# Token order of q in a linear-attention and SoLU kernel: runs of eight tokens on 64 partitions per head

## The chip, the cores and the metric

The kernel runs on one core of one Trainium2 chip. A core has five engines with queues of their own: TensorE (PE, matrix products), VectorE (DVE), ScalarE (ACT), GpSimd (POOL) and SyncE (SP). SP, ACT and POOL can issue transfers, which 16 shared DMA engines carry out. Weight loads of PE (PEld) are recorded beside its products. The metric is the time of one execution on the device, in microseconds (us), lower is better.

## What is computed

The inputs are q, k and v of 8 batches, 8 heads, 576 tokens and 64 values each, a norm weight, and the two matrices of an expert layer. Everything is float32 in and out.

```python
# attention without a softmax, then a norm over the 64 values of each head
kv  = np.einsum('bhsd,bhse->bhde', k, v)
out = np.einsum('bhsd,bhde->bhse', q, kv)
rms = np.sqrt(np.mean(out * out, axis=-1, keepdims=True) + 1e-06)
attn = out / rms * g_norm
# tokens x (heads * 64) = 4608 x 512, through 512 -> 1024 -> 512
x = attn.transpose(0, 2, 1, 3).reshape(B * S, H * D)
h = x @ w_in
sm = np.exp(h - h.max(-1)) / sum(...)
solu = h * sm
ln = (solu - mean(solu)) / sqrt(var(solu) + 1e-06) * g_ln
y = ln @ w_out
```

Every token passes through the two parts by itself, apart from kv, which sums over all tokens of its batch and head. So the order in which tokens sit in the kernel's chunks is free, as long as each row of the output ends up at its own place.

## The kernel before

**Chunks.** The 4608 tokens are worked in nine chunks of 512. Chunks c = 0 to 7 hold tokens 0 to 511 of batch c. Chunk 8 holds the last 64 tokens of all eight batches. The feature dimension lies on the partitions for the expert layer, the tokens on the free dimension.

**Loading.** `load_kv` (line 213) brings k and v of a batch as bf16: a pair of heads fills the 128 partitions, 64 for each, and a partition holds nine tokens that follow each other. `load_q` (line 222) brings tokens 0 to 511 of q with 128 partitions, each holding four tokens of every head (`j=4`). `load_q_last` (line 230) brings the last 64 tokens of one batch, on every eighth partition of the tile `q_last`. All these are issued by POOL, which casts on the way. Batches 0 and 1 are loaded in two halves of four heads.

**Attention.** `kv_mm` (line 280) forms kv from k and v, `kv_copy` brings it to SBUF as `kvd`, once straight and once with the two halves of the partitions exchanged. q has to be transposed, so that head values lie on partitions: for chunks 0 to 3 by `qT_mm` (line 313), eight 128x128 products against an identity per half, with `qT_copy`; for chunks 4 to 8 (`XBAR`) by `q_turn` (line 330), one DMA transpose issued by SP. A transposed block of 128 rows holds two tokens: z = 0 on partitions 0 to 63, z = 1 on the others. `o_mm` (line 337) forms q times kv for half the heads (`hf`), with two results (z) of 512 columns. For chunks 0 to 7 that is eight products of 256 columns per half. For chunk 8 it is 64 products of 32 columns per half, since each batch needs its own kv and its columns are every eighth one. Then come a square (`o_sq`), the mean over a head by a product (`s_mm`), the root (`s_ln`, `s_exp`) and the scaling `x_mul`.

**Expert layer.** For every chunk `h_mm` makes eight blocks of h (four products of 512 columns each), `h_exp` (ACT) and `h_u` (DVE) the exponential and the product with it. POOL and ACT make the squares and sums that `sums` (PE) reduces. `out_mm` (line 578) makes four blocks of 128 tokens by 512 outputs, in half steps of four products; `scale` (line 609) multiplies by the row's factor and writes `ob`, of which there are four buffers in turn; `store` (line 616) sends 128 rows of 2 KB out. Stores go on SP's queue, except that in chunk 8 block 1 goes on ACT's. Block 3 of chunk 8 is made in two column halves (`out_cols`, `scale_cols`, `store_cols`, lines 587 to 607), one stored by SP and one by ACT.

**The order of the work** is written by a planner (`Plan`, line 19). Every piece is given an engine, a cost, a rank (a due time), what it needs and which buffers it takes. `order` then picks, again and again, the piece that could start first by these costs, and by rank among equals. The engines run their lists strictly in that order. So a changed cost or rank, as in `plan.add(("q_last", b), ...)` (line 266), can move other pieces too. The SP list before is: four stores of chunk 0, the transpose of chunk 4, three stores of chunk 1, the transpose of chunk 5, four stores, that of 6, three stores, that of 7, four stores, that of 8, and the other stores.

Of the kernel before, what the change touches and what calls it, by code (L numbers as in the profile page):

```python
# [8 lines left out]
FP32 = mybir.dt.float32  # L9
FP32R = mybir.dt.float32r  # L10
BF16 = mybir.dt.bfloat16
# [78 lines left out]
def kernel(  # L90
# [20 lines left out]
    nc = tc.nc  # L111
    B, H, S, D = q.shape
# [34 lines left out]
    kvd = big.tile([128, B, 2, NP, D], BF16, name="kvd")  # L147
    q_last = big.tile([128, H, 4, D], BF16, name="q_last")
    g_rep = big.tile([128, 1], FP32, name="g_rep")
# [62 lines left out]

    def load_kv(name, src, b, hs):

        if hs.start == 0:
            T[name, b] = tile_of((name, b), [128, NP, 9, D], BF16)
        nc.gpsimd.dma_start(  # L217
            T[name, b].rearrange("p n i d -> p n (i d)")[:, hs.start // 2:hs.stop // 2],
            src[b, hs].rearrange("(n r) (p i) d -> (r p) n (i d)", r=2, i=9),
        )  # L220

    def load_q(b, hs):
        if hs.start == 0:
            T["q", b] = tile_of(("q", b), [128, H, 4, D], BF16)
        nc.gpsimd.dma_start(  # L225
            T["q", b].rearrange("p h j d -> p h (j d)")[:, hs],
            q[b, :, 0:512, :].rearrange("h (p j) d -> p h (j d)", j=4)[:, hs],
        )

    def load_q_last(b):  # L230
        nc.gpsimd.dma_start(
            q_last[b:128:B].rearrange("p h j d -> p h (j d)"),
            q[b, :, 512:S, :].rearrange("h (p j) d -> p h (j d)", j=4),
        )

# [16 lines left out]
    for b in range(B):  # L252
        at = b - 9.0 if b > 1 else (-2.0, -1.5)[b]
        behind = [] if b < 2 else [("h_mm", 0, 0)] if b == 2 else [("h_mm", b - 3, 2 if b == 3 else 0)]
        for g, hs in enumerate(heads(b)):
            part = 0.1 * g
            n = len(heads(b))
            for i, (name, src) in enumerate((("k", k), ("v", v))):
                plan.add((name, b, g), "pool", 0.75 if n == 1 else 0.6, at + part + 0.01 * i,
                         lambda name=name, src=src, b=b, hs=hs: load_kv(name, src, b, hs),  # L260
                         behind, uses=[(name, b)] if g else [],
                         first=[] if g else [(name, b)], load=2.9 / n if b < 3 else 3.5)
            plan.add(("q", b, g), "pool", 0.9 if n == 1 else 0.7, at + part + (0.02 if b < 2 else 0.1),
                     lambda b=b, hs=hs: load_q(b, hs), behind,
                     uses=[("q", b)] if g else [], first=[] if g else [("q", b)], load=2.7 / n if b < 3 else 3.3)
        plan.add(("q_last", b), "pool", 0.6, 2.0 + 0.5 * b, lambda b=b: load_q_last(b),
                 [("h_mm", 2 + b // 2, 4 * (b % 2))], load=0.5)
    for half in range(2):
# [44 lines left out]
    def qT_mm(c, hf, tag):  # L313

        t = T["qTp", c, hf] = bank((tag,), [128, 4, 2, 128], BF16)
        for h in range(4):
            for y in range(2):
                src = T["q", c][:, 4 * hf + h, 2 * y:2 * y + 2, :].rearrange("p z d -> p (z d)")
                nc.tensor.transpose(t[:, h, y, :], src, ident[:, :])

    def qT_copy(c, hf):
        if hf == 0:
            T["qT", c] = tile_of(("qT", c), [128, H, 2, 128], BF16)
        dst, src = T["qT", c][:, 4 * hf:4 * hf + 4], T["qTp", c, hf][:, :, :, :]
        if c == 1:
            nc.scalar.copy(dst, src)
        else:
            nc.vector.tensor_copy(dst, src)

    def q_turn(c):  # L330

        t = T["qT", c] = tile_of(("qT", c), [128, H, 2, 128], BF16)
        nc.sync.dma_start_transpose(
            t.rearrange("q h y p -> q (h y) p"), T["q", c].rearrange("p h j d -> p (h j d)")
        )

    def o_mm(c, hf, tag):

        ts = [bank((tag,), [128, 2, 2, 128], FP32) for z in range(2)]
        for z in range(2):  # L340
            T["o", c, hf, z] = ts[z]
        for pp in range(2):
            for b in [c] if c < B else range(B):
                cols = slice(0, 128) if c < B else slice(b, 128, B)
                for hh in range(2):
                    for z in range(2):
                        rows = slice(64 * z, 64 * z + 64)
                        nc.tensor.matmul(  # L348
                            ts[z][hh * 64:hh * 64 + 64, pp, :, cols], kvd[rows, b, hh ^ z, 2 * hf + pp, :],
                            T["qT", c][rows, 4 * hf + 2 * pp + hh, :, cols], start=True, stop=True,  # L350
                        )
# [23 lines left out]
    def s_exp(*i):  # L375
        t = T["rst", i] = tile_of(("rst", i), [128, 2, 2, 128], FP32)
        nc.scalar.activation(  # L377
            out=t.rearrange("p a b c -> p (a b c)"), in_=T["lss", i][:, :], func=AF.Exp, scale=-0.5, bias=zero_t[:, :]
        )

    def s_rsqrt(*i):
        t = T["rst", i] = tile_of(("rst", i), [128, 2, 2, 128], FP32)
        nc.scalar.activation(
            out=t.rearrange("p a b c -> p (a b c)"), in_=T["s", i][:, :], func=AF.Abs_reciprocal_sqrt, bias=eps_t[:, :]
        )

    def x_mul(c, hf, z):
        if (hf, z) == (0, 0):
            T["x", c] = tile_of(("x", c), [128, NP, 2, 2, 128], BF16)
        nc.vector.scalar_tensor_tensor(  # L390
# [6 lines left out]
    for c in range(NC):  # L397
# [19 lines left out]
        for hf in range(2):  # L417
            g = group(c, hf)
            tag = ("out", "h")[c] if c < 2 and hf else "o"
            if c not in XBAR:  # L420
# [8 lines left out]
            kvs = [("kv", b, x, part) for b in ([c] if c < B else range(B)) for x in ((hf,) if b < 2 else range(2)) for part in range(3)]  # L429
            plan.add(("o_mm", c, hf), "pe", 0.25 if c < B else 1.2, r + w * (0.35 + 0.5 * hf),  # L430
                     lambda c=c, hf=hf, tag=tag: o_mm(c, hf, tag), [("qT", c) if c in XBAR else ("qT", c, hf), *kvs],
# [173 lines left out]
    def store_cols(x):  # L605
        dst = out.rearrange("(b s) (x d) -> b s x d", b=B, x=2)[:, 512:S, x, :].rearrange("b (p j) d -> j p b d", j=4)[3]
        (nc.sync, nc.scalar)[x].dma_start(dst, T["ob", NC - 1, 3][:, x])

    def scale(c, m):
# [3 lines left out]
        else:  # L613
            nc.vector.tensor_scalar_mul(out=t[:, :], in0=T["acc", c, m][:, :], scalar1=T["rstd", c][:, m:m + 1])  # L614

    def store(c, m):
        j = 2 * (m % 2) + m // 2
        if c < B:
            dst = out[c * S:c * S + 512, :].rearrange("(p j) d -> j p d", j=4)
        else:  # L620
            dst = out.rearrange("(b s) d -> b s d", b=B)[:, 512:S, :].rearrange("b (p j) d -> j p b d", j=4)

        (nc.scalar if c == NC - 1 and m % 2 else nc.sync).dma_start(dst[j], T["ob", c, m][:, :])

# [65 lines left out]
```

## Time and profile before

| | us |
|---|---|
| median of 6 runs | 196.23 |
| lowest and highest of them | 195.36, 205.79 |
| the profiled execution | 195.36 |
| its span, first to last instruction | 193.6 |
| PE busy | 180.5 |
| ACT busy | 141.1 |
| POOL busy | 128.0 |
| DVE busy | 122.3 |

The granted TensorE clock was 1.0 throughout. Busy time of PE is modelled with overlapping ends, so the time that a group of products holds PE is better read from its start to the start of the next group. The chain that ended last gives 27% of the span to `out_mm` (L582) and 25% to `h_mm` (L468).

What the loads look like from POOL's side and on the DMA queues:

```profile
L225 POOL DMA_DIRECT2D q_sb<-in_q_dram x10 | 8.6, 856 | 2.5 <-DMA w_in_sb<-in_moe_w_in_dram 1.4
```

```profile
q0 software_dynamic: 20112, 17.30, 56.6%
q1 hardware_dynamic: 15616, 11.67, 23.1%
```

The first row is a group of instructions: line, engine, operation, tile, count, then busy time, mean ns of one, idle time before it and what ended most of it. The next two are the DMA queue of POOL (q0) and that of SP (q1): packets, megabytes, share of the 16 engines' span.

```profile
out_dram<-ob_sb SPq DMA_DIRECT2D x34, 256.0 KB, 3.1
q_sb<-in_q_dram POOLq DMA_DIRECT2D x6, 512.0 KB, 16.0
q_last<-in_q_dram POOLq DMA_DIRECT2D x8, 64.0 KB, 10.0
qT_sb<-q_sb SPq DMA_TRANSPOSE x4, 9.6
```

These rows are transfers: how many, KB each, and the median us from issue to landing.

### The profile page before, as it was taken

How to read it: one execution, taken by the hardware profiler on the slowest of the kernel's cores; microseconds unless marked ns; L12 is line 12 of the kernel's file. 1: busy time of each engine (PE TensorE's matmuls, PEld its weight loads, DVE VectorE, ACT ScalarE, POOL GpSimd, SP SyncE). 2: the span in 40 equal slices, each digit the busy share in tenths (PEclk: the TensorE clock that was granted, in tenths of full speed). 3: DMA queues.
4: the chain of work that ended last, by engine and by line, in shares of the span. 5: the costliest groups of instructions: out<-in, count | busy, mean ns of one | idle time of the engine just before them, and what ended most of it. 6: DMA issues, size and time to landing. Idle time of an engine off the chain costs nothing.

```text
span 193.6 us, 5442 instructions
## 1 busy us (share of the span) xinstructions
PE 180.5 (93%) x2282; PEld 88.7 (46%) x2282; DVE 122.3 (63%) x241; ACT 141.1 (73%) x245; POOL 128.0 (66%) x136
## 2 busy tenths in 40 slices
PE   7987997997999998999799999999999999999991
PEld 2442454652354533544254435445445554544460
DVE  1356588478684886496377668577575747666450
ACT  2028888879895996899588987979789496655420
POOL 7982699400999986977489776568385838846200
PEclk9999999999999999999999999999999999999999
DMA  3999999999995999999999997353111111211206
GB/s 47 193 203 279 342 203 206 205 224 254 228 205 83 128 164 268 134 175 185 274 214 195 210 82 208 113 102 129 54 54 58 58 54 58 108 58 54 110 11 210
DMA packets 36040, 29.71 MB, mean 153 GB/s; under 512 B 11816, under 2 KB 30512, under 8 KB 36016
## 3 DMA queue, kind: packets, MB, share of 16 engines
q0 software_dynamic: 20112, 17.30, 56.6%
q1 hardware_dynamic: 15616, 11.67, 23.1%
q8 instruction: 18, 0.29, 0.6%
q10 hardware_dynamic: 288, 0.39, 0.6%
q14 instruction: 6, 0.05, 0.1%
HBM read 32.51 MB, written 9.44 MB: 217 GB/s over the span
## 4 chain that ended last, share of the span: by engine, by line
PE 71%; ACT 9%; DMA 8%; DVE 4%; POOL 3%; issue 2%; SPq 0%; POOLq 0%; DVEq 0%
PE out_ps L582 27%; PE h_ps L468 25%; PE misc_ps L534 4%; DMA out_dram<-ob_sb 4%; DMA v_sb<-in_v_dram 4%; PE s_ps L369 3%; PE o_ps L348 3%; ACT e_sb L476 2%; PE misc_ps L291 2%; DVE u_sb L483 2%; ACT osq_sb L363 2%; ACT rst_sb L377 1%; ACT lss_sb L373 1%; POOL k_sb L217 1%; DVE w_out_sb L573 1%
## 5 line engine op out<-in xcount | busy, mean ns | idle before, releaser
L468 PE MATMUL h_ps<-x_sb,w_in_sb 128*128 128x512 bf16 x276 | 70.3, 379 | 2.8 <-DVE u_sb L483 1.5
L582 PE MATMUL out_ps<-w_out_sb,u_sb 128*128 128x512 bf16 x272 | 69.1, 379 | 0.7 <-issue 0.7
L494 POOL TENSOR_TENSOR usq_sb<-u_sb 128x512 bf16<-128x512 bf16 x50 | 52.0, 1043 | 26.6 <-DVE u_sb L483 26.5
L483 DVE TENSOR_TENSOR u_sb<-h_ps,e_sb 128x512 bf16<-128x512 f32 x69 | 47.4, 689 | 30.3 <-ACT e_sb L476 29.4
L500 POOL TENSOR_TENSOR es_sb<-e_sb 128x512 bf16<-128x512 f32 x36 | 45.9, 1274 | 21.8 <-ACT e_sb L476 21.4
L476 ACT ACTIVATE e_sb<-h_ps,zero_t 128x512 f32<-128x512 f32 x69 | 47.2, 685 | 12.5 <-PE h_ps L468 11.6
L468 PEld LDWEIGHTS <-w_in_sb 128*128 128x128 bf16 x288 | 27.3, 98 | 37.3 <-issue 6.7
L582 PEld LDWEIGHTS <-u_sb 128*128 128x128 bf16 x280 | 26.1, 98 | 31.6 <-issue 2.7
L363 ACT ACTIVATE osq_sb<-o_ps,zero_t 128x512 bf16<-128x512 f32 x31 | 20.2, 684 | 15.7 <-PE o_ps L348 15.7
L614 DVE TENSOR_SCALAR ob_sb<-out_ps,rstd 128x512 f32<-128x512 f32 x33 | 24.6, 746 | 10.7 <-PE out_ps L582 4.5
L390 DVE SCALAR_TENSOR_TENSOR x_sb<-o_ps,g_rep,rst_sb 128x512 bf16<-128x512 f32 x32 | 23.9, 749 | 8.6 <-ACT rst_sb L377 8.4
L377 ACT ACTIVATE rst_sb<-lss_sb,zero_t 128x512 f32<-128x512 f32 x32 | 23.2, 726 | 0.7
L373 ACT ACTIVATE lss_sb<-s_ps,eps_t 128x512 f32<-128x512 f32 x32 | 22.0, 689 | 2.0 <-PE s_ps L369 1.9
L492 ACT ACTIVATE usq_sb<-u_sb,zero_t 128x512 bf16<-128x512 bf16 x22 | 15.8, 719 | 5.4 <-DVE u_sb L483 5.4
L369 PE MATMUL s_ps<-osq_sb,head_mean 128*128 128x512 bf16 x34 | 12.9, 380 | 0.6 <-ACT osq_sb L363 0.6
L534 PEld LDWEIGHTS <-stat_sel 128*32 128x32 bf16 x720 | 10.1, 97 | 3.8 <-issue 3.8
L198 PE MATMUL s_ps<-zeros 128*128 128x512 bf16 x28 | 9.9, 480 | 1.4 <-DVE zero_t L163 1.2
L217 POOL DMA_DIRECT2D k_sb<-in_k_dram x10 | 7.8, 785 | 3.6 <-DMA w_in_sb<-in_moe_w_in_dram 2.2
L225 POOL DMA_DIRECT2D q_sb<-in_q_dram x10 | 8.6, 856 | 2.5 <-DMA w_in_sb<-in_moe_w_in_dram 1.4
L348 PE MATMUL o_ps<-qT_sb,kvd 64*64 64x32 bf16 (+1 forms) x240 | 8.2, 256 | 1.8 <-DMA qT_sb<-q_sb 1.3
L291 PEld LDWEIGHTS <-k_sb 64*64 64x64 bf16 x576 | 6.8, 107 | 4.0 <-issue 4.0
L348 PEld LDWEIGHTS <-kvd 64*64 64x64 bf16 x256 | 4.6, 114 | 8.3 <-issue 7.3
(85 smaller groups left out, 134.7 us busy)
## 6 DMA issues: line engine op xcount, KB each, us to landing
out_dram<-ob_sb SPq DMA_DIRECT2D x34, 256.0 KB, 3.1
k_sb<-in_k_dram POOLq DMA_DIRECT2D x6, 576.0 KB, 14.1
v_sb<-in_v_dram POOLq DMA_DIRECT2D x6, 576.0 KB, 14.7
q_sb<-in_q_dram POOLq DMA_DIRECT2D x6, 512.0 KB, 16.0
w_out_f<-in_moe_w_out_dram POOLq DMA_DIRECT2D x1, 2048.0 KB, 15.8
k_sb<-in_k_dram POOLq DMA_DIRECT2D x4, 288.0 KB, 11.2
v_sb<-in_v_dram POOLq DMA_DIRECT2D x4, 288.0 KB, 11.9
q_sb<-in_q_dram POOLq DMA_DIRECT2D x4, 256.0 KB, 11.9
```

What stands on the lines that cost most here:

```text
L363: nc.scalar.activation(out=t[:, :], in_=T[("o", *i)].rearrange("p a b c -> p (a b c)"), func=AF.Square, bias=zero_t[:, :])
L369: nc.tensor.matmul(t[:, :], head_mean[:, :], T["osq", i][:, :], start=True, stop=True)
L373: nc.scalar.activation(out=t[:, :], in_=T["s", i][:, :], func=AF.Ln, bias=eps_t[:, :])
L377: nc.scalar.activation(out=t.rearrange("p a b c -> p (a b c)"), in_=T["lss", i][:, :], func=AF.Exp, scale=-0.5, bias=zero_t[:, :])
L390: nc.vector.scalar_tensor_tensor(out=T["x", c][:, 2 * hf:2 * hf + 2, z], in0=T["o", c, hf, z][:, :, :, :], scalar=g_rep[:, :], in1=T["rst" ...
L468: nc.tensor.matmul(t[:, :], w_in_sb[:, dt, f * 128:(f + 1) * 128], T["x", c][:, dt].rearrange("p a b c -> p (a b c)"), start=(dt == 0), st ...
L476: nc.scalar.activation(out=T["e", c, f // 2][:, f % 2, :], in_=T["h", c, f][:, :], func=AF.Exp, bias=zero_t[:, :])
L483: nc.vector.tensor_tensor(out=T["u", c][:, f, :], in0=T["h", c, f][:, :], in1=T["e", c, f // 2][:, f % 2, :], op=MUL)
L494: nc.gpsimd.tensor_tensor(out=dst, in0=src, in1=src, op=MUL)
L500: nc.gpsimd.tensor_tensor(out=T["es", c][:, n, :], in0=e[:, 0, :], in1=e[:, 1, :], op=ADD)
L582: nc.tensor.matmul(T["acc", c, m][:, :], T["u", c][:, f, m * 128:(m + 1) * 128], w_out_sb[:, f, :], start=(f == 0), stop=(f == NF - 1),)
L614: nc.vector.tensor_scalar_mul(out=t[:, :], in0=T["acc", c, m][:, :], scalar1=T["rstd", c][:, m:m + 1])
```

## The change

q is now laid out as k and v are: a pair of heads fills the partitions, 64 for each, and a partition holds eight tokens that follow each other; one `load` serves all three. The ninth token of every partition goes to chunk 8. There, the batch stands where the token of the run stood before: `q_last[:, :, b, :]`, one token of each partition and head pair for each batch. `o_mm` takes four runs of 64 columns instead of two of 128; in chunk 8 it makes 32 products of 64 columns per half, where y and z name the batch. The loads of last tokens become due late (rank 4.0 + 0.25 b) and wait for later steps of `h_mm`. A block of 128 rows of the output now holds two tokens of every run (for chunk 8: two batches), and each store is two of 64 rows.

```diff
-    q_last = big.tile([128, H, 4, D], BF16, name="q_last")
+    q_last = big.tile([128, NP, B, D], BF16, name="q_last")
...
+    def load(name, src, b, hs):
+        js = 8 if name == "q" else 9
         if hs.start == 0:
-            T[name, b] = tile_of((name, b), [128, NP, 9, D], BF16)
+            T[name, b] = tile_of((name, b), [128, NP, js, D], BF16)
         nc.gpsimd.dma_start(
+            T[name, b].rearrange("p n j d -> p n (j d)")[:, hs.start // 2:hs.stop // 2],
+            src[b, hs].rearrange("(n r) (p j) d -> (r p) n (j d)", r=2, j=9)[:, :, 0:js * D],
         )
-    def load_q(b, hs):
-        if hs.start == 0:
-            T["q", b] = tile_of(("q", b), [128, H, 4, D], BF16)
-        nc.gpsimd.dma_start(
-            T["q", b].rearrange("p h j d -> p h (j d)")[:, hs],
-            q[b, :, 0:512, :].rearrange("h (p j) d -> p h (j d)", j=4)[:, hs],
-        )
     def load_q_last(b):
-        nc.gpsimd.dma_start(
-            q_last[b:128:B].rearrange("p h j d -> p h (j d)"),
-            q[b, :, 512:S, :].rearrange("h (p j) d -> p h (j d)", j=4),
-        )
+        nc.gpsimd.dma_start(q_last[:, :, b, :], q[b].rearrange("(n r) (p j) d -> (r p) n j d", r=2, j=9)[:, :, 8, :])
...
-        plan.add(("q_last", b), "pool", 0.6, 2.0 + 0.5 * b, lambda b=b: load_q_last(b),
-                 [("h_mm", 2 + b // 2, 4 * (b % 2))], load=0.5)
+        plan.add(("q_last", b), "pool", 0.7, 4.0 + 0.25 * b, lambda b=b: load_q_last(b),
+                 [("h_mm", 4 + b // 4, 2 * (b % 4))], load=0.7)
...
-            for b in [c] if c < B else range(B):
-                cols = slice(0, 128) if c < B else slice(b, 128, B)
+            n = 2 * hf + pp
+            for y in [slice(0, 4)] if c < B else range(4):
                 for hh in range(2):
                     for z in range(2):
                         rows = slice(64 * z, 64 * z + 64)
                         nc.tensor.matmul(
-                            ts[z][hh * 64:hh * 64 + 64, pp, :, cols], kvd[rows, b, hh ^ z, 2 * hf + pp, :],
-                            T["qT", c][rows, 4 * hf + 2 * pp + hh, :, cols], start=True, stop=True,
+                            ts[z][hh * 64:hh * 64 + 64, pp, y, :], kvd[rows, c if c < B else 2 * y + z, hh ^ z, n, :],
+                            T["qT", c][rows, n, y, 64 * hh:64 * hh + 64], start=True, stop=True,
                         )
...
     def store_cols(x):
-        dst = out.rearrange("(b s) (x d) -> b s x d", b=B, x=2)[:, 512:S, x, :].rearrange("b (p j) d -> j p b d", j=4)[3]
-        (nc.sync, nc.scalar)[x].dma_start(dst, T["ob", NC - 1, 3][:, x])
+        cols = slice(x * d_model // 2, (x + 1) * d_model // 2)
+        for y in range(2):
+            (nc.sync, nc.scalar)[x].dma_start(
+                rows_of(NC - 1, 1, 2 + y)[:, cols], T["ob", NC - 1, 3][64 * y:64 * y + 64, x]
+            )
...
+    def rows_of(c, z, y):
+        if c < B:
+            return out[c * S:c * S + S, :].rearrange("(p j) d -> j p d", j=9)[2 * y + z]
+        return out.rearrange("(b p j) d -> j b p d", p=64, j=9)[8, 2 * y + z]
     def store(c, m):
-        j = 2 * (m % 2) + m // 2
...
-        (nc.scalar if c == NC - 1 and m % 2 else nc.sync).dma_start(dst[j], T["ob", c, m][:, :])
+        for x in range(2):
+            (nc.scalar if c == NC - 1 and m % 2 else nc.sync).dma_start(
+                rows_of(c, m // 2, 2 * (m % 2) + x), T["ob", c, m][64 * x:64 * x + 64, :]
+            )
```

The planner's costs follow: a q load counts 0.8 for POOL instead of 0.9 and 2.55 for DMA instead of 2.7 (3.2 instead of 3.3 from batch 3 on), half loads of q count 0.6 instead of 0.7, and the products of chunk 8 count 0.6 a half instead of 1.2. In the order that comes out, the last tokens' loads follow batch 7's loads, the loads of batches 5 and 6 stand one POOL instruction earlier, the transpose of chunk 6 stands one store earlier on SP and that of chunk 8 two stores later, and the steps of PE are mixed differently from chunk 1's end on.

## The prediction

> **What bounds the kernel now.** I read four views. First the page's slices and the table of busy time by stretch:
>
> ```profile
> PE   7987997997999998999799999999999999999991
> DMA  3999999999995999999999997353111111211206
> ...
> 88.00:96.00 8.00, 6.69 (x39) 2.88 (x37) 4.18 (x7) 5.76 (x9) 4.97 (x5) 1.00 1.29 216
> ...
> 112.00:128.00 16.00, 16.00 (x229) 7.74 (x230) 11.28 (x23) 14.28 (x26) 10.25 (x11) 1.00 0.60 116
> ...
> 144.00:160.00 16.00, 16.00 (x267) 8.38 (x265) 10.04 (x19) 12.02 (x22) 9.43 (x9) 1.00 0.14 51
> ```
>
> Columns of the last three: stretch, length, busy time (count) of PE, weight loads, DVE, ACT, POOL, granted clock, DMA share, GB/s. There are two regimes. Up to about 100 us the DMA engines are full (the 9s) and PE has holes. From 112 us on PE is busy without a hole while DMA falls to 0.60 and then 0.14. So after 100 us only TensorE work counts; before it, what DMA brings, and when, counts too.
>
> Second, the timeline of PE around the last chunk, with a kv product for comparison:
>
> ```profile
> 53.84 0.22 PE L291 MATMUL misc_ps<-v_sb,k_sb 64*64 64x64 bf16 x2
> ...
> 54.55 1.90 PE L468 MATMUL h_ps<-x_sb,w_in_sb 128*128 128x512 bf16 x8
> ...
> 144.83 1.13 PE L348 MATMUL o_ps<-qT_sb,kvd 64*64 64x32 bf16 x64
> 145.89 1.04 PE L582 MATMUL out_ps<-w_out_sb,u_sb 128*128 128x512 bf16 x4
> ```
>
> PE time is read from start to next start. The 64 small products of the last chunk's first half hold PE for 145.89 - 144.83 = 1.06 us (16.6 ns each), the second half 1.07 us (154.67 to 155.74). The 72 products of a kv step, with the same 64x64 weights and twice the columns, take 54.55 - 53.84 = 0.71 us: 9.9 ns each.
>
> Third, the chain of waits and the timeline at the one large hole:
>
> ```profile
> 86.94 0.50 SPq L333
> 87.53 8.33 DMA out_dram<-ob_sb
> 95.96 0.75 DVE ob_sb L614
> ```
>
> ```profile
> 80.53 6.90 SPq L333 DMA_TRANSPOSE qT_sb<-q_sb  x1
> 95.57 0.41 PE L348 MATMUL o_ps<-qT_sb,kvd 64*64 64x256 bf16 x8 [1.31 <-DMA qT_sb<-q_sb]
> ```
>
> Batch 5's DMA transpose could start only at 80.53, when q of batch 5 (issued at 62.82) had landed. It held SP for 6.90 us, and its data came at about 95.5, because k, v and q of batch 6 (issued from 78.34 on) share the engines. The product that needs it waited. A store behind it on SP took 8.33 us and held an output buffer. Eight output matmuls before that product took 95.57 - 92.37 = 3.20 us where eight take 1.73 elsewhere: 1.5 us lost.
>
> Fourth, ACT at the end:
>
> ```profile
> 187.59 0.69 ACT L612 ACTIVATE ob_sb<-out_ps,rstd 128x512 f32<-128x512 f32 x1 [1.12 <-PE out_ps L582]
> 188.31 0.63 ACTq L623 DMA_DIRECT2D out_dram<-ob_sb  x1
> 189.29 0.47 ACT L603 ACTIVATE ob_sb<-h_ps,rstd 128x256 f32<-128x256 f32 x1 [1.01 <-PE h_ps L592]
> 189.79 0.56 ACTq L607 DMA_DIRECT2D out_dram<-ob_sb  x1
> ```
>
> The last store leaves ACT's queue at 189.79 and lands 2.7 us later; the span ends at 193.6.
>
> **The change part by part.**
>
> *Last chunk's products.* Before, each of 8 batches has its own 16 tokens in two groups, 128 products of 32 columns read with a stride of 8. Now y runs over 4 and z picks the batch, so there are 64 products of 64 adjoining columns. Upper price: 32 a half at today's 16.6 ns is 0.53 us, saving 2 x 0.53 = 1.06 us. Lower price: 32 at the kv rate of 9.9 ns is 0.32 us, saving 2 x 0.75 = 1.5 us. I take 1.5: the kv row has the new form exactly (64x64 weights, 64 adjoining columns, all four quadrants in turn). Nothing covers it, as PE has no hole there: -1.5 us. For the other chunks the 256 columns become four runs of 64 instead of two of 128; the sums step reads runs of 32 at the usual rate, so nothing is added (if it slowed them by 10%, 16 steps of 0.34 us would cost 0.5 us).
>
> *Loads of q.* A half load goes from 512 pieces of 1 KB to 256 of 2 KB, a whole one from 1024 to 512. One half of q (512 pieces, 32 for each of 16 engines) took 13.41 - 12.03 = 1.38 us, from the landing of v in the chain to the end of PE's wait for q: 43 ns for a piece of 1 KB. k and v of the same half, 32 pieces of 2.25 KB per engine, came in the 3.0 us left of the 4.4 us between the two first kv steps (7.62 and 12.07), at most 95 ns each. A piece of 2 KB then costs 75 to 86 ns, and a whole q load shrinks by 0 to 0.4 us of about 8 us per batch. I take 0.2. At the start two halves stand ahead of the first expert matmul: -0.1 us. POOL's own issue (856 ns a q load) shrinks by some 0.1, hidden in its idle time.
>
> *Last tokens.* Eight loads move from between batches 5 to 7's loads to behind batch 7's, and each goes from 128 pieces (1 KB read, 512 B written) to 512 pieces (256 B read, 128 B written). The total goes from 1024 to 4096. On POOL an issue with 512 pieces takes 0.78 us (the half q loads) against 0.56: 8 x 0.22 = 1.8 us more, in a stretch where POOL is busy 10.25 of 16 us. Behind it wait squares and sums whose results are needed a chunk later: nothing, and up to 0.5 us if they become late. On DMA no row has 128 B writes. Nearest are the transposes: queue q1's 15616 packets less 4608 store rows leave some 2200 for each of five, 137 per engine, and the last one, with the engines nearly to itself, landed in 4.3 us: at most 31 ns a packet. So 32 x 31 ns = 1.0 us a load, 8 us in all. The Trainium skill, "DMA: Bandwidth & Descriptors", Specifications, speaks against it: a transfer below 512 B is a read-modify-write and misses line rate. If that doubled the price the eight would take 16 us. They fall between about 98 and 130 us, where DMA has a third of its time free, and the last transpose was issued at 127.42 and not needed until 144.83. I take the trace's price and zero on the path; the slack of 13 us is the cover, and beyond it each microsecond of landing is one of PE.
>
> *The planner.* The printed order shows that batch 5's and 6's loads each move ahead of a POOL square (1.0 us earlier); batch 6's transpose goes ahead of one store, and the last one behind two. Batch 5's first product comes after 23 half output steps instead of 25: PE asks for batch 5's transpose 2 x 0.865 = 1.7 us earlier in its work. Against that, q of batch 5 lands earlier: 1.0 (issue), 0.2 to 1.1 (three smaller q loads in the backlog before it, itself, no last tokens). And batch 6's loads are shorter under the transpose: no last tokens (2 x 128 pieces, 0.7 us), q less 0.2. Sum 1.9 to 3.0 earlier against 1.7: the 1.5 us hole stays or loses up to 1.3. I take -0.3.
>
> *Stores as two of 64 rows.* SP's issues go from 37 to 72. A 332 ns median each is 12 us more on a queue whose longest waits are for data (118.0 us for DVE): hidden. The Trainium skill, same page, Rules for kernel authors, says that two transfers to disjoint partition halves aren't worth making, since both use the same engines and serialize. By that rule the pair lands as one would, and only issue time is added; the row here for a whole store is 3.1 us to landing. I keep 0 before the end. At the end it is not hidden. ACT issues the second half of chunk 8's store 1 at 188.94, till about 189.5, so its last scaling starts at 189.5, not 189.29: +0.25. Then two issues of 0.56 instead of one: +0.56. Less some 0.1 for a half-size landing: +0.7 us (+0.3 if an issue costs SP's 332 ns).
>
> **Sum.** -1.5 -0.1 -0.3 +0.7 = -1.2 us. The profiled execution took 195.36 (span 193.6 and 1.8 around it), so 194.2 in its terms; it is the fastest of the six, whose median is 196.23. On the median: 195.0.
>
> **The rivals.**
>
> *Transpose late (slower).* Place: batch 5's first product, and by the same gear batch 6's. It is asked for 1.7 us earlier while its landing doesn't move, because transposes, not loads, fill the engines (14.9 us to landing at worst). For: 6.90 us on SP. Against: fewer pieces. Hole 3.2 instead of 1.5 at each of one or two batches, so +1.7 to +3.4 in place of -0.3: 197 to 199 us. It decides once q of batch 5 lands less than 0.2 us earlier than 80.5.
>
> *Relief.* With 1 us less DMA per batch, the 1.5 us hole closes and so do half of those between 66 and 74 us (0.4 + 0.4 + 0.9): -1.5 - 0.8 in place of -0.3: 193.0. For: DMA is full there. Against: 66 to 74 waits for ACT and DVE in the chain.
>
> *Last tokens late.* At over 100 ns a piece each load takes 3.2 us or more, 26 us in all, and delays batch 7's and the last transpose beyond 144.8: +3, 198 us. Against: the slack.
>
> *No saving:* the last chunk's products take as long as before (limited by their PSUM side): 196.5.
>
> **How the numbers follow.** Forecast 0.36 (194 to 196.2), relief 0.23, transpose late 0.25, last tokens late 0.10, none 0.06. Faster by over 1% (below 194.3; 1% is about what can be told from no change): nearly all of relief and an eighth of the forecast, 0.26. Slower by over 1% (above 198.2): half of transpose late and of last tokens late, 0.18. Within 1%: 0.56. The range 192.3 to 198.9 leaves out a fifth of relief and the far ends of the two late cases; the likeliest case alone is 194 to 196.2.
>
> **What would show it.** The last chunk's two o_ps groups at 0.3 us start to start (0.5 or 1.06: wrong price); PE's wait at batch 5's first product against 1.31 us, and SP's transpose of it before 80.5; last-token loads landing within 10 us and the last transpose before 144; two issues of ACT at the end and its last scaling delayed. The forecast is wrong if PE shows a new wait after 100 us, or if the holes between 40 and 75 us change by more than 1 us through the new order.

## The result, and the profile after

The changed kernel takes 193.24 us, the median of 28 runs (192.78 to 204.67), the kernel before 195.62 us, the median of 65. The ratio is 0.9913, with an interval of 0.9897 to 0.9928: 1.7 us or 0.9% faster. Ratios here, with 95% intervals, compare only runs within 1.5% of their kernel's fastest; slower ones, most of them with a granted clock of 0.98 to 0.99 in the records, are left out, and the kernel before has more of these (up to 205.79 us). The time lies within the range of the prediction, 1.8 us below the forecast of 195.0 and just below the 194 to 196.2 of its likeliest case. By the ratio it falls in the likeliest class, within 1%; by the medians, which are 1.2% apart, and by the prediction's own limit of 194.3 us, it is one class faster. The profiled execution took 193.02 (span 191.3) against 195.36 (span 193.6).

The page first: the slices of PE and DMA, the DMA queues of POOL (q0) and SP (q1), and three rows of transfers.

```profile
PE   7998896997899999999999999999999999999980
...
DMA  3999999999995999999799993556624022414335
...
q0 software_dynamic: 19088, 17.30, 54.5%
q1 hardware_dynamic: 16176, 11.68, 26.2%
...
out_dram<-ob_sb SPq DMA_DIRECT2D x68, 128.0 KB, 3.0
...
q_sb<-in_q_dram POOLq DMA_DIRECT2D x6, 512.0 KB, 13.4
```

From the twelfth slice on PE shows only nines but for the last two; before, an 8 stood in the 16th and a 7 in the 20th, the one with the large hole. DMA keeps its two regimes, but the second is fuller in slices 26 to 30 (120 to 143 us), the time in which the last of the last tokens and their transpose now come. A q load lands in 13.4 us instead of 16.0.

The same stretches as before, of the table of busy time by stretch (length, PE, weight loads, DVE, ACT, POOL, granted clock, DMA share, GB/s):

```profile
88.00:96.00 8.00, 8.00 (x45) 3.47 (x43) 5.49 (x9) 7.33 (x13) 6.49 (x7) 1.00 0.73 188
...
112.00:128.00 16.00, 16.00 (x230) 7.62 (x229) 11.44 (x23) 13.43 (x26) 12.60 (x14) 1.00 0.50 93
```

The stretch of the large hole, 6.69 us of PE in 8 before, is now full.

PE's timeline at batch 5's first product and at the last chunk's two halves:

```profile
91.00 1.03 PE L455 MATMUL h_ps<-x_sb,w_in_sb 128*128 128x512 bf16 x4
91.95 0.41 PE L335 MATMUL o_ps<-qT_sb,kvd 64*64 64x256 bf16 x8
...
145.17 0.45 PE L335 MATMUL o_ps<-qT_sb,kvd 64*64 64x64 bf16 x32
145.55 1.04 PE L455 MATMUL h_ps<-x_sb,w_in_sb 128*128 128x512 bf16 x4
...
152.60 0.45 PE L335 MATMUL o_ps<-qT_sb,kvd 64*64 64x64 bf16 x32
152.98 0.82 PE L455 MATMUL h_ps<-x_sb,w_in_sb 128*128 128x512 bf16 x3
```

The product at 91.95 has no bracket: nothing is waited for. A half of the last chunk holds PE 0.38 us from start to start, against 1.06 and 1.07. And ACT at the end:

```profile
184.12 0.69 ACT L602 ACTIVATE ob_sb<-out_ps,rstd 128x512 f32<-128x512 f32 x1 [1.12 <-PE out_ps L569]
184.84 1.22 ACTq L615 DMA_DIRECT2D out_dram<-ob_sb  x2
186.18 0.47 ACT L590 ACTIVATE ob_sb<-h_ps,rstd 128x256 f32<-128x256 f32 x1 [1.37 <-PE h_ps L579]
186.68 1.23 ACTq L595 DMA_DIRECT2D out_dram<-ob_sb  x2
```

Both stores of ACT are two issues now. The last issue ends at about 187.9, and the span ends 5.1 us after the start of the last scaling, 4.3 before.

**Where the 2.3 us of the two spans are.** Call the middle the time from the first expert product to the start of the last 28 output products. It is 166.95 us before (17.79 to 184.74) and 163.34 after (17.93 to 181.27): -3.61. Of that the last chunk is -1.37, and the hole at batch 5 some -1.8 (it was 3.20 us for eight output products that take 1.73, and 0.35 more just behind). The other -0.4 is the balance of small ones: 0.42 and 0.36 us at 66 and 70 us, which every profile with the old order on PE has, are gone, and so is one of 0.87 at 72.28, which the second profile of the kernel before does not have either; 0.55 at 58.28 and 0.45 in the kv step at 68.51, which every profile with the new order has, came; the rest are smaller. Single profiles differ by as much: a second one of each kernel, below, has a middle of 166.28 and 163.34, so -2.94. The start adds 0.14. From the last 28 products to the last scaling it is 4.91 us instead of 4.55, +0.36, and from there to the end +0.8. Sum: -3.61 + 0.14 + 0.36 + 0.8 = -2.3.

### The profile page after: what moved, and what is told of

Same layout as the page of the kernel before. It is cut to its first block, busy times and chain, and to the rows that moved or that the text cites. A ratio compares the mean times of both kernels' runs of the same rounds, so it can differ in the third digit from the quotient of the medians.

```text
span 191.3 us, 5359 instructions
## 1 busy us (share of the span) xinstructions
PE 179.1 (94%) x2218; PEld 87.8 (46%) x2218; DVE 122.6 (64%) x241; ACT 141.2 (74%) x245; POOL 128.6 (67%) x136
## 4 chain that ended last, share of the span: by engine, by line
PE 77%; ACT 8%; DMA 4%; DVE 4%; POOL 3%; issue 1%; ACTq 1%; POOLq 0%
PE out_ps L569 30%; PE h_ps L455 28%; PE misc_ps L521 5%; DMA v_sb<-in_v_dram 4%; PE s_ps L356 3%; PE o_ps L335 2%; ACT rst_sb L364 2%; PE misc_ps L278 2%; ACT lss_sb L360 2%; DVE x_sb L377 2%; ACT osq_sb L350 2%; POOL k_sb L218 1%; DVE w_out_sb L560 1%; PE misc_ps L198 1%; DVE u_sb L470 1%
## 5 line engine op out<-in xcount | busy, mean ns | idle before, releaser
L481 POOL TENSOR_TENSOR usq_sb<-u_sb 128x512 bf16<-128x512 bf16 x50 | 51.9, 1044 | 24.6 <-DVE u_sb L470 24.5
L604 DVE TENSOR_SCALAR ob_sb<-out_ps,rstd 128x512 f32<-128x512 f32 x33 | 24.4, 746 | 6.3 <-ACT rstd L548 3.5
L218 POOL DMA_DIRECT2D q_sb<-in_q_dram x10 | 7.5, 751 | 3.1 <-DMA w_in_sb<-in_moe_w_in_dram 1.4
L278 PE MATMUL misc_ps<-v_sb,k_sb 64*64 64x64 bf16 x360 | 7.9, 194 | 0.1
L296 DVE CAST kvd<-misc_ps 64x128 bf16<-64x128 f32 (+1 forms) x24 | 6.9, 287 | 1.6 <-PE misc_ps L278 1.4
## 6 DMA issues: line engine op xcount, KB each, us to landing
q_sb<-in_q_dram POOLq DMA_DIRECT2D x6, 512.0 KB, 13.4
v_sb<-in_v_dram POOLq DMA_DIRECT2D x4, 288.0 KB, 11.9
```

Source lines behind the costliest of these rows:

```text
L481: nc.gpsimd.tensor_tensor(out=dst, in0=src, in1=src, op=MUL)
```

## The experiments

Two theories stood for the closed hole. *Layout*: smaller or fewer pieces make the loads shorter. *Order*: what counts is when the transpose on SP and the next batch's loads on POOL are issued relative to each other. They could be told apart because the planner's costs, which set the order, can be changed without the layout.

**Order alone, layout alone.** The first kernel is the one before with the planner's numbers of the one after, the second the reverse.

```diff
-            plan.add(("q", b, g), "pool", 0.9 if n == 1 else 0.7, at + part + (0.02 if b < 2 else 0.1),
+            plan.add(("q", b, g), "pool", 0.8 if n == 1 else 0.6, at + part + (0.02 if b < 2 else 0.1),
...
-                     uses=[("q", b)] if g else [], first=[] if g else [("q", b)], load=2.7 / n if b < 3 else 3.3)
+                     uses=[("q", b)] if g else [], first=[] if g else [("q", b)], load=2.55 / n if b < 3 else 3.2)
...
-        plan.add(("q_last", b), "pool", 0.6, 2.0 + 0.5 * b, lambda b=b: load_q_last(b),
-                 [("h_mm", 2 + b // 2, 4 * (b % 2))], load=0.5)
+        plan.add(("q_last", b), "pool", 0.7, 4.0 + 0.25 * b, lambda b=b: load_q_last(b),
+                 [("h_mm", 4 + b // 4, 2 * (b % 4))], load=0.7)
...
-            plan.add(("o_mm", c, hf), "pe", 0.25 if c < B else 1.2, r + w * (0.35 + 0.5 * hf),
+            plan.add(("o_mm", c, hf), "pe", 0.25 if c < B else 0.6, r + w * (0.35 + 0.5 * hf),
```

> The kernel before (q in runs of four, stores of 128 rows) with the changed planner's numbers, so that every engine's list of steps is that of the changed kernel. Theory A (the hole at batch 5's first product goes through the order: earlier loads of batches 5 and 6, late last tokens): the wait of 1.3 us there is gone, the span falls by 1.5 to 2 us, ratio to before 0.990 to 0.993; the last chunk's products stay at 1.06 us each. Theory B (it goes through the smaller number of pieces of q): the hole stays, or grows to some 3 us as the product is asked for 1.7 us earlier, ratio 1.00 to 1.01.

> The changed kernel with the planner's numbers of before, so that every engine's list of steps is that of before, the last tokens' loads early. Theory A (order): the hole at batch 5's first product stays at 1.3 us or more; left are the products of the last chunk (-1.4 us) and the longer end (+0.8 us), ratio to before 0.995 to 1.000. Theory B (fewer pieces of q): the hole is gone all the same, ratio 0.988 to 0.992. A third possibility: eight last-token loads of 512 small pieces in the full stretch make the hole larger, ratio above 1.003.

| kernel | median | ratio | span | middle |
|---|---|---|---|---|
| before | 195.62 | 1 | 193.6 | 166.95 |
| order alone | 193.80 | 0.9977 (0.9929 to 1.0025) | 191.7 | 165.03 |
| layout alone | 194.03 | 0.9953 (0.9916 to 0.9991) | 192.1 | 163.68 |
| both (after) | 193.24 | 0.9913 (0.9897 to 0.9928) | 191.3 | 163.34 |

By its ratio, order alone is not told from no change. Neither kernel reaches the ratio that was forecast for the theory that its profile fits (0.990 to 0.993 and 0.988 to 0.992). So the hole is followed in the profiles.

Order alone keeps 1.07 us a half of the last chunk and takes 1.92 us off the middle, about what the hole is worth. Layout alone takes 3.27 off: 1.37 of the last chunk, and again 1.9, although its order is the old one. Neither of their profiles has a wait at batch 5's first product. Both together take 3.61. So the hole is closed by either and counted once. That speaks against *layout* as the only cause, and the order of issue needs a finer look. The starts of SP's transpose of batch 4 and POOL's loads of batch 5, in the timeline of the kernel before:

```profile
61.11 1.69 SPq L333 DMA_TRANSPOSE qT_sb<-q_sb  x1
...
61.28 0.81 POOL L217 DMA_DIRECT2D k_sb<-in_k_dram  x1
62.09 0.75 POOL L217 DMA_DIRECT2D v_sb<-in_v_dram  x1
62.82 0.90 POOL L225 DMA_DIRECT2D q_sb<-in_q_dram  x1
```

with layout alone:

```profile
60.85 1.73 SPq L320 DMA_TRANSPOSE qT_sb<-q_sb  x1
...
62.00 0.80 POOL L218 DMA_DIRECT2D k_sb<-in_k_dram  x1
```

and after the change, where the order on POOL puts the loads a square (1.0 us) earlier:

```profile
60.11 0.80 POOL L218 DMA_DIRECT2D k_sb<-in_k_dram  x1
...
60.41 7.56 SPq L320 DMA_TRANSPOSE qT_sb<-q_sb  x1
...
75.09 2.92 SPq L320 DMA_TRANSPOSE qT_sb<-q_sb  x1
...
76.39 0.81 POOL L218 DMA_DIRECT2D k_sb<-in_k_dram  x1
```

The columns are start, duration, instruction. Now the landing. In the list of transfers cut to one issue, the transpose of batch 4 reads, before:

```profile
qT_sb<-q_sb SPq DMA_TRANSPOSE x1, 11.6
```

with layout alone:

```profile
qT_sb<-q_sb SPq DMA_TRANSPOSE x1, 3.7
```

and after:

```profile
qT_sb<-q_sb SPq DMA_TRANSPOSE x1, 14.6
```

Issued 1.15 us ahead of the loads, it lands in 3.7 us. Issued 0.3 us behind, it waits for them and lands in 14.6, at 75.0; PE asks for it at 76.03, so that costs nothing. Issued 0.17 us ahead, both suffer: 11.6 us, and the q load behind it takes 17.7 us (62.82 to 80.5) against 13.0 (layout alone) and 12.7 (after). In the kernel before, the late q then makes the transpose of batch 5 late: it starts at 80.53, *behind* the loads of batch 6 (78.34), and lands 14.9 us later, at 95.4. After the change it starts at 75.09, ahead of those loads at 76.39, and is never waited for. (Its landing was not recorded.)

What put the transpose ahead in layout alone? The loads of batch 5 start 43.5 us after the first expert product in both kernels (61.28 - 17.79 and 62.00 - 18.51). The transpose starts 43.3 us after it in the kernel before, but 42.3 with layout alone, because q of batch 4, which it waits for, lands sooner. The load of that q reads, before:

```profile
q_sb<-in_q_dram POOLq DMA_DIRECT2D x1, 512.0 KB, 24.8
```

and with layout alone:

```profile
q_sb<-in_q_dram POOLq DMA_DIRECT2D x1, 512.0 KB, 23.8
```

Over all profiles it takes 24.4 to 25.4 us with the old pieces (six) and 23.8 to 24.5 with the new (seven), 24.8 and 24.2 on the mean. So *layout* has a part after all: with the new pieces this q lands some 0.7 us sooner, and that can move a transpose out of the collision.

**The kernel before once more**, to see whether the hole repeats.

> The kernel before, unchanged, for a second profile. If the wait at batch 5's first product belongs to the kernel: PE waits there again for 1 us or more, q of batch 5 lands some 17 us after its issue, and the transpose of batch 4 and the k load of batch 5 are issued within 0.3 us of each other. If it belongs to the one execution: no wait, and q of batch 5 lands within 14 us.

It does: 195.61 us, span 193.8. The eight output products took 3.23 us, with a wait of 1.3. The transposes were issued 0.09 us ahead of and 3.0 us behind the loads, and landed in 13.4 and 13.8 us; q of batch 5 took 17.9 us.

**Moving batch 5's loads**, and nothing else. In the kernel before they and one last-token load are put behind a later POOL square, so that the transpose of batch 4 is well ahead of them. In a second kernel, the new layout with the old planner's numbers, they are put ahead of an earlier one, ("usq", 1, 7), so that they meet the transpose with the new pieces. The edit of the first:

```diff
...
-    for fn in plan.order():
+    steps = plan.order()
+    moved = [(name, 5, 0) for name in "kvq"] + [("q_last", 0)]
+    taken = [step for step in steps if step[0] in moved]
+    steps = [step for step in steps if step[0] not in moved]
+    at = [n for n, _ in steps].index(("usq", 2, 0)) + 1
+    for _, fn in steps[:at] + taken + steps[at:]:
```

> The kernel before, with the loads of batch 5 (and of the first last tokens) moved one POOL square later, behind the first of chunk 2. Collision theory (a DMA transpose that is issued just ahead of the loads takes 12 us and makes them late; one with the engines to itself for a microsecond or more lands in 3.7): batch 4's transpose lands within 5 us, q of batch 5 within 14 us of its issue, earlier than 80.5 in spite of the later issue, the wait at batch 5's first product falls from 1.3 us to at most 0.5, and the span by 1 to 1.9 us; ratio 0.990 to 0.996. Order theory (the loads must come earlier): q of batch 5 lands at 82 or later, the wait grows by 1.5 us or more, ratio 1.005 to 1.01.

195.33 us, ratio 1.0057 (1.0017 to 1.0096); by the medians, 195.33 against 196.2 for the kernel before beside it, it is the other way round, so neither a gain nor a loss is shown. The first half of the reason held: the transpose of batch 4 (61.66, loads at 65.08) landed in 3.8 us and q of batch 5 in 13.4. The forecast of the time did not. q was issued 3.8 us later, so it landed at 80.0, and the transpose of batch 5 still came behind batch 6's loads:

```profile
78.72 0.83 POOL L217 DMA_DIRECT2D k_sb<-in_k_dram  x1
...
80.06 7.86 SPq L333 DMA_TRANSPOSE qT_sb<-q_sb  x1
...
95.62 0.41 PE L348 MATMUL o_ps<-qT_sb,kvd 64*64 64x256 bf16 x8 [1.32 <-DMA qT_sb<-q_sb]
```

A miss that sharpens the theory: the hole hangs on the *second* pair, transpose 5 against loads 6. The first collision matters only because it makes that transpose late.

> The changed kernel with the planner's numbers of before (no hole in its profile), and the loads of batch 5 one POOL square earlier, so that they are issued within some 0.3 us of batch 4's transpose, as in the kernel before. Collision theory: the transpose takes 11 us or more again; if it is issued first, q of batch 5 lands 16 us or more after its issue and PE waits at batch 5's first product; if the loads are first, they land within 14 us and the transpose late, at some 75 us, just in time for batch 4's first product. Theory of fewer pieces: the loads land in 13 us and the transpose in less than 6.

195.58 us, ratio 1.0047 (0.9996 to 1.0098). Loads at 60.88 and transpose at 61.07: 15.9 us to landing, with the new pieces. So smaller or fewer pieces do not shorten a transpose that stands behind the loads; the expectation of under 6 us is refuted. The transpose came behind the loads, not just ahead of them, so that case was not met with the new pieces. PE waited elsewhere: the loads now stand ahead of a POOL square that the sums of chunk 1 need, and PE waited 0.94 us for it, until 65.03.

**Moving batch 6's loads** behind the transpose of batch 5, in the kernel before. The edit is the one above with 6 for 5, last tokens of batch 2, and ("usq", 3, 1).

> The kernel before, with the loads of batch 6 (and of the third last tokens) moved three POOL steps later, behind the second square of chunk 3, so that they are issued some microseconds after batch 5's transpose and not 2 us ahead of it. If the wait at batch 5's first product comes from the transpose standing behind batch 6's loads: the transpose, issued at 80 to 82 still, lands in under 8 us instead of 14 to 15, the wait is gone, the span falls by 1.5 to 2 us, ratio 0.988 to 0.994. If the late landing of q of batch 5 (80.5) sets it: the wait stays at 1.3 us, ratio 0.998 to 1.002.

197.60 us, ratio 1.0096 (1.0038 to 1.0153). The hole at batch 5 is gone, as the theory has it: the transpose (78.04, loads at 83.15) landed in 4.7 us. But the time went up by 1% (by the medians 197.60 against 196.26), where it should have gone down. In this execution the transpose of batch 4 (61.72) came 0.39 us behind the loads (61.33) and landed in 16.8 us, which cost 1.91 us at batch 4's first product; and with everything on POOL later, batch 7's loads now stood ahead of batch 6's transpose:

```profile
97.19 0.83 POOL L217 DMA_DIRECT2D k_sb<-in_k_dram  x1
...
98.26 7.42 SPq L333 DMA_TRANSPOSE qT_sb<-q_sb  x1
...
113.57 0.41 PE L348 MATMUL o_ps<-qT_sb,kvd 64*64 64x256 bf16 x8 [2.31 <-DMA qT_sb<-q_sb]
```

It landed in 15.3 us, and PE lost 2.47 us. The wait moved by one batch, with the same cause.

**What the last chunk's products cost.** Two kernels take apart stride and number. One has the new layout, with 64 products of 32 adjoining columns in the place of 32 of 64. The other is the kernel before with adjoining columns in place of every eighth (there the last tokens meet another batch's kv, so the values of chunk 8 are changed).

```diff
-            for y in [slice(0, 4)] if c < B else range(4):
+            wide = 64 if c < B else 32
+            for y, w in [(slice(0, 4), 0)] if c < B else [(y, w) for y in range(4) for w in (0, 32)]:
...
```

```diff
-                cols = slice(0, 128) if c < B else slice(b, 128, B)
+                cols = slice(0, 128) if c < B else slice(16 * b, 16 * b + 16)
```

> The changed kernel with each product of the last chunk made as two of 32 adjoining columns: 64 products a half as before, but no stride in the columns. If the saving came from the number of products: 1.06 us a half again, 1.4 us slower than the changed kernel. If it came from the stride of the columns: 0.55 to 0.65 us a half (some 9 ns each), 0.4 to 0.5 us slower than the changed kernel.

> The kernel before, where each batch's columns of the last chunk are 16 adjoining ones of each half and not every eighth; so tokens of the last chunk meet the kv of other batches. If the stride of the columns sets the price: the 64 products a half take 0.62 to 0.70 us instead of 1.06, as the 64 without stride did in the changed layout. If their number or form of two short runs does: 1.06 us as before.

The new layout cut to 32 columns, 193.83 us, ratio 0.9943 (0.9913 to 0.9973):

```profile
145.56 0.76 PE L336 MATMUL o_ps<-qT_sb,kvd 64*64 64x32 bf16 x64
146.25 0.82 PE L456 MATMUL h_ps<-x_sb,w_in_sb 128*128 128x512 bf16 x3
```

The old layout without its stride, 193.82 us in one execution:

```profile
144.00 0.69 PE L348 MATMUL o_ps<-qT_sb,kvd 64*64 64x32 bf16 x64
144.62 0.61 PE L582 MATMUL out_ps<-w_out_sb,u_sb 128*128 128x512 bf16 x2
```

Start to start that is 0.69 and 0.62 us (the second halves take 0.62 and 0.62). The 64 products cost 1.06 us with a stride of eight and 0.62 without: 16.6 against 9.7 ns each. Half as many of twice the width then cost 0.38: 11.9 ns each. Of 0.68 us saved a half, 0.44 is the stride and 0.24 the number. The stride goes in two places at once, in the tile that the products read (`qT`) and in the PSUM tile that they write (`o_ps`). Which of the two costs the time was not taken apart.

**The end.** ACT's second halves are issued by POOL, which is idle there.

```diff
-            (nc.sync, nc.scalar)[x].dma_start(
+            ((nc.sync, nc.scalar)[x] if y == 0 or x == 0 else nc.gpsimd).dma_start(
...
-            (nc.scalar if c == NC - 1 and m % 2 else nc.sync).dma_start(
+            (nc.sync if c < NC - 1 or not m % 2 else (nc.scalar, nc.gpsimd)[x]).dma_start(
```

> The changed kernel with the second half of each of ACT's last stores issued by POOL, which has nothing left to do. If the two issues on ACT cost 0.6 to 0.8 us at the end: the time from ACT's last scaling to the end of the span falls from 5.1 us to 4.3 to 4.6 us, ratio to the changed kernel about 0.997. If landing sets the end whatever the issue: no change. If a transfer issued by POOL lands later than one by ACT: 0.3 to 1 us slower.

ACT's end and SP's last issue of this kernel:

```profile
184.89 0.58 ACTq L615 DMA_DIRECT2D out_dram<-ob_sb  x1
185.87 0.47 ACT L590 ACTIVATE ob_sb<-h_ps,rstd 128x256 f32<-128x256 f32 x1 [1.01 <-PE h_ps L579]
186.37 0.50 ACTq L595 DMA_DIRECT2D out_dram<-ob_sb  x1
...
186.50 1.29 SPq L595 DMA_DIRECT2D out_dram<-ob_sb  x2
```

The last scaling is no longer held up: 4.55 us after the start of the last 28 products, as in the kernel before, not 4.91. But SP still issues two stores, until 187.8, and the end comes 4.8 us after the scaling: 0.3 of the 0.8 is won. 192.96 us, ratio 0.9889 (0.9834 to 0.9945), span 190.7. A further kernel gave POOL the second halves of chunk 8's first three stores and one half of the last:

> The changed kernel with the second half of each of chunk 8's first three stores and one half of the last issued by POOL, so that neither ACT nor SP has two issues ahead of the last ones. If issues are what makes the end longer: SP's last two issues stand at some 4.2 us after the start of the last 28 output products instead of 5.2, the span ends 0.8 to 1.1 us earlier than the changed kernel's, ratio to before 0.985 to 0.989. If POOL's transfers are later to land or land in each other's way: no better than 0.3 us.

193.65 us, ratio 0.9887 (0.9813 to 0.9962). Its profiled execution took 201.35 us (span 199.6, granted clock 0.982), so it can't be read for the end. Beside them, the changed kernel once more:

> The changed kernel, unchanged, for a second profile and beside the next one: no wait at batch 5's first product, 0.38 us a half for the last chunk's products, 5.1 us from ACT's last scaling to the end of the span; ratio 0.989 to 0.993.

193.43 us, 0.9899 (0.9842 to 0.9956), with 0.38 us a half, no wait at batch 5, and 5.1 us from last scaling to end. The intervals of the three overlap: a gain from the third queue is seen in the one span, not shown in the time.

## Why the prediction came out as it did

**Last chunk's products: right mechanism, size nearly right.** Forecast -1.5 us, measured -1.37. The lower price (the kv row's 9.9 ns) was the right one to take, but the new products take 11.9 ns. The upper price, today's 16.6 ns, failed because most of that was the stride, which the change removes: the row of the old form was no bound for the new one.

**Loads of q: small, as said, but not without effect.** At the start the forecast was -0.1 us, the first expert product came 0.14 later: too small to be told. The median landing (13.4 us against 16.0) says little, as kernels with old pieces and no collision had 13.3 and 13.4 for batch 5's too. But q of batch 4, at the end of a backlog of loads, landed 0.7 us sooner on the mean, of the size of the 0.2 to 1.1 that the prediction gave to smaller loads ahead of q of batch 5. In layout alone that put the transpose ahead of the next loads.

**Last tokens: right.** Zero on the path. The last transpose, issued at 131.49, landed at 136.4 and was needed at 145.17. A load holds each engine for 1.04 us (last section), against the 1.0 us that the prediction took from the transposes' packets. That was an upper bound from another kind of transfer, so its closeness is in part luck. The doubled price of 2 us did not come.

**The planner: this step failed.** It gave the hole at batch 5's first product -0.3 us, and it is worth -1.8. The prediction set an earlier demand (1.7 us) against an earlier landing (1.9 to 3.0 us) made up of an earlier issue and smaller transfers. Each term was a small shift in a steady queue. But the landing did not shift by 2 us: q of batch 5 came at 74.4 instead of 80.5 and the transpose was issued 5.4 us earlier (75.09 for 80.53), on the other side of batch 6's loads. What decides is which comes first, transpose or loads, and by how much: a step of some 11 us of landing (3.7 to 14.6) over 1.5 us of issue (1.15 ahead to 0.3 behind). The prediction named the collision with batch 6's loads when it read the hole, then priced it as a share of bandwidth.

**Stores: right mechanism, too small.** Forecast +0.25 for the last scaling held up by a second issue of ACT, +0.56 for the second of the last two issues, -0.1 for a landing of half the size: +0.7. Measured +0.36 and +0.8, together +1.2. Two issues took 1.22 us where one had taken 0.56 and 0.63, and the smaller store did not land sooner: from the end of ACT's last issue to the span's end it was 3.2 us before (190.35 to 193.6) and 3.4 after (187.91 to 191.3). The kernel with the third queue shows the 0.36 to be that second issue. Elsewhere the doubled issues hid, as said: a half store lands in 3.0 us where a whole one took 3.1, and PE has no wait of over 0.3 us after 60 us.

**Sum.** Forecast -1.5 -0.1 -0.3 +0.7 = -1.2; measured -1.37 + 0.14 - 1.8 - 0.4 + 1.2 = -2.2 by these rounded terms, -2.3 in spans, -1.7 by the ratio. So the forecast had about half of the gain. Another 0.6 us of the 1.8 between 195.0 and 193.24 is its base: the median of six runs was 196.23, that of 65 is 195.62. That the range held, and by the ratio the class, is in part luck: the gain that was missed at the hole (1.5 us) and the price at the end (0.5 more than forecast) partly offset each other. The time lies nearest to the rival *Relief* (193.0), which had the hole close. Its reason, less DMA per batch, is enough in layout alone, through the order of transpose and loads, but it is not needed: order alone closes the hole with the old pieces. The holes between 66 and 74 us, of which it had half close, went as well, against new ones of 0.55 and 0.45. *Transpose late* did not occur here, but it is real: in the kernel with batch 6's loads moved it cost 1.91 and 2.47 us, at just the kind of place that it named. The changed order is near it too: the transpose of batch 4 lands only 1.0 us before it is needed, and in the kernel with 32 columns, in the same order, PE waited 0.27 us for it. In the execution of 201.35 us above, PE even waited 3.84 us for the transpose of batch 6, issued 3.0 us behind batch 7's loads. Neither sign of being wrong came: PE has no wait of over 0.2 us after 100 us, and the holes between 40 and 75 us changed by some -0.6 in all.

**What stays open.** The transpose of batch 6 landed in 6.7 to 7.9 us in four profiles with the old layout and order, though it stood 3.7 to 5.1 us ahead of the next loads; in seven others it took 3.6 to 4.9. The reason was not looked for. A version in which every transpose is pinned more than 1 us ahead of the next loads wasn't tried. The runs of the kernel before lie wider (most between 193 and 199 us) than those after (26 of 28 between 192.8 and 194.3). A collision that turns on tenths of a microsecond of issue would do that: in four profiles with this order and these pieces up to there, the transpose of batch 4 stood 0.6, 0.17 and 0.09 us ahead of the loads, and 0.39 behind. But no profile of one of its shortest or longest runs was taken, so this is argued only.

## What to carry to other kernels

When two queues feed the same DMA engines, look up for each dependent transfer which large transfers were issued just ahead of it; one place in that order can be worth ten microseconds of landing. The size of the pieces was worth 0.7 us here, and it mattered where it moved a transfer across such a place. Price the new form of an operation by a row that shares its access pattern, not by the old form: here the stride cost more than the count. And when an edit also changes a planner's costs, run layout and order apart: either closed the same hole, and adding both gains would have counted it twice.

## What the hardware did that was not expected

- *A DMA transpose against loads of the next batch (1.6 MB in three issues).* By the start of the transpose against the first of these loads, over all profiles here: 1.15 us or more ahead, it landed in 3.6 to 4.9 us in ten cases and in 6.7 to 9.2 in five; 0.6 ahead, in 7.1; 0.09 and 0.17 ahead, in 13.4 and 11.6, and the q load then took 17.9 and 17.7 us instead of about 13; behind them, in 13.8 to 16.8. SP was held 1.6 to 4.9 us by one that stood 1.15 us or more ahead and 6.2 to 9.1 us by one behind loads, with the stores queued after it.
- *Small pieces.* Last tokens in 512 pieces of 128 B landed in 4.2, 4.0, 2.8, 3.0 and 2.8 us once the engines had room; in the same order with 128 pieces of 512 B in 2.9, 4.3, 2.3, 3.4 and 2.3. That is 0.3 us more on the mean of five. The engines' time tells more. In the 4 us from 117 us on, with one such load in each, POOL's queue reads with 128 B and with 512 B:

```profile
q0 software_dynamic: 528, 0.07, 25.9%
```

```profile
q0 software_dynamic: 144, 0.07, 14.5%
```

That is 1.04 and 0.58 us of each engine for the same bytes, 1.8 times as much, or 31 and 64 ns a packet. The Trainium skill ("DMA: Bandwidth & Descriptors", Specifications) has a transfer below 512 B miss line rate as a read-modify-write. The loss of rate agrees; whether a read-modify-write makes it, no run here shows. POOL's issue grew too, from 0.56 to 0.80 us.

- *Strided columns.* 64x64x32 products cost 16.6 ns each with columns eight apart, in the tile read and in the PSUM tile written alike, and 9.7 ns with adjoining ones.
